# ELU's middle operation, one bit step of 16 weight pieces and a small copy moved to POOL in an attention and feed-forward kernel

## The chip, the cores and the metric

One NeuronCore of a Trainium2 chip. The time is that of one execution in device microseconds, from the first to the last instruction with what lies around it; the span in the profile is the part that the hardware profiler saw. Engines: PE multiplies matrices, DVE (VectorE), ACT (ScalarE) and POOL (GpSimd) work element by element, SP only issues transfers. Each engine takes its instructions strictly in the order in which they stand in its queue.

## The reference: windowed attention with sinks, then an ELU feed-forward layer

```python
# q, k, v: (4, 8, 768, 64); n_sink = 4, window = 128
keep = is_sink | ((rel >= 0) & (rel < window))
scores = where(keep, q @ k.T / sqrt(D), -1e9)
a = softmax(scores)            # per query row
x = (a @ v) as (3072, 512)     # 4 x 768 tokens, 8 heads x 64
h = x @ w_in                   # (3072, 2048)
g = where(h > 0, h, exp(min(h, 0)) - 1)
out = g @ w_out                # (3072, 512)
```

The weights w_in and w_out arrive as 64-bit floats.

## The kernel before: a planner writes the order of every engine

The 3072 tokens are 24 tiles of 128, in nine chunks (`SIZES`: three chunks of 2 tiles, then six of 3). Matrix products run in 16-bit floats with a high and a low part of each operand, so that one product becomes three.

**Attention** of a chunk goes head pair by head pair. PE makes the scores (L540, L541; L547 in chunks 0 and 1), DVE adds the mask and takes the row minimum (L566), ACT the exponential (L568), ACT and DVE the high and low part of the probabilities (L580, L581), POOL the four sink columns (L587 to L591), SP a transposing transfer (L599), and PE the product with v (L610, L615), from which ACT and DVE make the high and low part of x (L623, L624). v itself is split by ACT (L510) and DVE (L511); in chunks 1 to 8 ACT then copies eight rows of the low part to the place of the sinks' low part (L516).

**Weights** come in 32 pieces of 128x512; piece 2f is a column block f of w_in, piece 2f+1 the rows of w_out that belong to it. SP loads a piece as 64-bit words (L395). `weight_f32` makes 32-bit floats in four steps: ACT scales the high word (L267), DVE takes three low bits (L268), DVE the sign (L269), DVE puts all together (L270). ACT then makes the high part (L416) and POOL the low part (L417). A piece's load may be issued once the high part of the piece five before it is made (`AHEAD`).

**Feed-forward**: for each f PE makes h from x in 12 matmuls (L651, `stage1`). ACT takes exp (L659), DVE does `(e - 1) * G` (L661, ELU's middle operation), DVE takes min with 0 and max with h, which frees the bank of h (L662), ACT makes the high part of g (L664), POOL the low part (L665), and PE multiplies by w_out (L672, `stage2`), two values of f later (`LAG`). There are two banks of h. Chunks 0 and 1 run the first eight f, then both the second eight (`PARTS`), so that pieces 0 to 15 are needed first, pieces 16 to 31 only when the second halves begin. There are 9 x 16 = 144 values of f in all.

At the end, DVE checks the range of all numbers (`in_range`), PE sums the verdict over partitions (L741), DVE decides (`decide`), and all engines read the flag (L968) and branch past a general path.

**Order**: every step is a task with an engine, a planned duration and its predecessors. PE's order is fixed by positions (`pos`); from it each other task gets a due time, and a list scheduler (`Plan.forward`) puts on each engine whichever ready task is due first. `keep_order` then pins that order. So a changed duration or engine changes the order of all engines except PE. The planner models no interference between engines.

Of the kernel before, what the change touches and what calls it, by code (L numbers as in the profile page):

```python
# [15 lines left out]
AF = mybir.ActivationFunctionType  # L16
ALU = mybir.AluOpType
# [3 lines left out]
P = 128  # L21
# [71 lines left out]
class Plan:  # L93
# [162 lines left out]

def weight_f32(nc, v, d, u, raw):

    ui = u.bitcast(U16).rearrange("p (f t) -> p f t", t=2)
    words = raw.rearrange("p (f t) -> p f t", t=2)
    halves = raw.bitcast(U16).rearrange("p (f t) -> p f t", t=4)
    return (
        lambda: nc.scalar.activation(d, words[:, :, 1].bitcast(F32), AF.Copy, scale=2.0**-111),  # L267
        lambda: nc.vector.tensor_scalar(ui[:, :, 0], halves[:, :, 1], 13, None, ALU.logical_shift_right),  # L268
        lambda: nc.vector.tensor_scalar(ui[:, :, 1], halves[:, :, 3], 0x8000, None, ALU.bitwise_and),  # L269
        lambda: nc.vector.scalar_tensor_tensor(v.bitcast(I32), d.bitcast(I32), 3, u, ALU.logical_shift_left, ALU.bitwise_or),  # L270
    )
# [52 lines left out]
def fast_path(tc, ctx, first, kq, vx, wt, out, nw, flag):  # L324
# [65 lines left out]
    def weights(k):  # L390
        raw, v = raws[slot("raw")], wv[slot("wv")]

        def load():
            if wide:
                nc.sync.dma_start(raw, wt[k].bitcast(I32))  # L395
            else:
                nc.sync.dma_start(raw[:, :512].bitcast(F32), wt[k])

        def step(i):
            return lambda: weight_f32(nc, v, acc[2], wu[k % RINGS["wu"]], raw)[i]()  # L400

        ld = add("SP", 0.4, load, deps=[w_done.get(k - AHEAD, [None])[0]], lat=dma_us(P * 512 * 8))
        if wide:
            a = add("ACT", act_us(512), step(0), deps=[ld])
            u1 = add("DVE", 0.65, step(1), deps=[ld])
            u2 = add("DVE", 0.7, step(2), deps=[ld])
            b = add("DVE", 0.7, step(3), deps=[a, u1, u2])
            ring("wu", [u1, u2], [b])
            ring("wps", [a], [b])
            ring("raw", [ld], [a, u1, u2])  # L410
            first_acc2.append(b)
        else:
            a = b = add("ACT", act_us(512), lambda: nc.scalar.activation(v, raw[:, :512].bitcast(F32), AF.Copy, scale=W_SCALE), deps=[ld])
            ring("raw", [ld], [a])

        th = add("ACT", act_us(512), lambda: nc.scalar.activation(w[k][:, 0, :], v, AF.Copy), deps=[b])  # L416
        tl = add("POOL", 1.5, lambda: nc.gpsimd.tensor_tensor(w[k][:, 1, :], v, w[k][:, 0, :], ALU.subtract), deps=[th])  # L417
        ring("wv", [b], [tl])
        w_done[k] = th, tl

# [31 lines left out]
    def attention(c):  # L452
# [46 lines left out]
        for p in range(NP):  # L499
# [13 lines left out]
            ring("vs", [ld or va], [va, vb])  # L513
            if far:

                vb = add("ACT", 0.3, lambda vhi=vhi, vlo=vlo: nc.scalar.activation(vhi[64:72, nk * P :], vlo[64:72, nk * P :], AF.Copy), deps=[vb])  # L516
            ring("vhl", [va], v_users)

            po = po_ps[slot("po")]
# [114 lines left out]
    def feed_forward(c, f0, f1, start):  # L634
# [4 lines left out]
        for f in range(f0, f1):  # L639
            hp = h_ps[slot("h")]  # L640
            gf = gs[slot("g")][:, :n]
            i = slot("gh")
            gh, gl = ghs[i], gls[i]

            def stage1(hp=hp, f=f):
                win = w[2 * f].rearrange("p t (a f) -> p t a f", a=ND)
                k = 0
                for d in range(ND):
                    xh, xl = x[d][:2]
                    for part, xx in ((0, xh), (1, xh), (0, xl)):  # L650
                        nc.tensor.matmul(hp[:, :n], win[:, part, d, :], xx[:, :n], start=k == 0, stop=k == 3 * ND - 1)  # L651
# [7 lines left out]
            a = add("ACT", act_us(n) + 0.06, lambda gf=gf, hp=hp, sums=sums: nc.scalar.activation(gf, hp[:, :n], AF.Exp, scale=1.0 / G_SCALE, accum_out=sums), deps=[s1])  # L659
            exps_done.append(a)  # L660
            b = add("DVE", 0.1 + 0.0008 * n, lambda gf=gf: nc.vector.tensor_scalar(gf, gf, -1.0, G_SCALE, ALU.add, ALU.mult), deps=[a])  # L661
            b = add("DVE", dve_us(n), lambda gf=gf, hp=hp: nc.vector.scalar_tensor_tensor(gf, gf, 0.0, hp[:, :n], ALU.min, ALU.max), deps=[b])  # L662
            ring("h", [s1], [b])
            th = add("ACT", act_us(n), lambda gf=gf, gh=gh: nc.scalar.activation(gh[:, :n], gf, AF.Copy), deps=[b])  # L664
            tl = add("POOL", pool_us(n), lambda gl=gl, gf=gf, gh=gh: nc.gpsimd.tensor_tensor(gl[:, :n], gf, gh[:, :n], ALU.subtract), deps=[th])  # L665

            def stage2(order, gl=gl, gh=gh, f=f):
                def run():
                    wout = w[2 * f + 1]
                    for k, i in order:  # L670
                        gg, part = ((gh, 0), (gh, 1), (gl, 0))[k]
                        nc.tensor.matmul(acc[i], gg[:, i * P : (i + 1) * P], wout[:, part, :], start=f == f0 and k == 0, stop=f == f1 - 1 and k == 2)  # L672
# [27 lines left out]
            saved[c, i] = sto  # L700
            evacs[i] = ev

    saved, exps_done = {}, []
    start = 0
    for c, f0, f1 in PARTS:
        if f0 == 0:
# [30 lines left out]
        nc.vector.tensor_tensor(flag, flag, some[:, 0:1], ALU.mult)  # L737

    sp = s_ps[slot("s")]
    a = add("DVE", 2.0, in_range, deps=seen + exps_done)  # L740
    b = add("PE", 0.1, lambda: nc.tensor.matmul(sp[:, 0:3], ones, some16, start=True, stop=True), deps=[a], pos=start + 2 * LAG - 1.5)  # L741
    ring("s", [b], [add("DVE", 0.6, decide, deps=[b])])
    for writer, users in later:
        writer.deps.extend(users)
# [252 lines left out]
```

## Time and profile before

| | us |
|---|---|
| time, median of 3 runs (660.2 to 663.14) | 660.67 |
| the profiled execution | 662.14 |
| its span | 660.3 |
| PE busy in the span | 609.9 |
| DVE, ACT, POOL busy in the span | 458.4, 456.9, 338.2 |

PE is the busiest engine, but not evenly: in 40 slices of the span it is at 3 to 8 tenths in the first eight, at 9 in nearly all of the rest. DVE is the other way around: 9 in most of the first six slices, then 6 or 7. The profile's busy shares are averages over these two stages, so that the prediction reads windows of the span rather than the totals. In a view of groups, a row gives line, engine, operation, output<-inputs, shapes and count, then busy time in us and the mean duration of one in ns, then the engine's idle time just before them and what ended it.

### The profile page before, as it was taken

How to read it: one execution, taken by the hardware profiler on the slowest of the kernel's cores; microseconds unless marked ns; L12 is line 12 of the kernel's file. 1: busy time of each engine (PE TensorE's matmuls, PEld its weight loads, DVE VectorE, ACT ScalarE, POOL GpSimd, SP SyncE). 2: the span in 40 equal slices, each digit the busy share in tenths (PEclk: the TensorE clock that was granted, in tenths of full speed). 3: DMA queues.
4: the chain of work that ended last, by engine and by line, in shares of the span. 5: the costliest groups of instructions: out<-in, count | busy, mean ns of one | idle time of the engine just before them, and what ended most of it. 6: DMA issues, size and time to landing. Idle time of an engine off the chain costs nothing.

```text
span 660.3 us, 13443 instructions
## 1 busy us (share of the span) xinstructions
PE 609.9 (92%) x4449; PEld 370.2 (56%) x4449; DVE 458.4 (69%) x1251; ACT 456.9 (69%) x1340; POOL 338.2 (51%) x497
## 2 busy tenths in 40 slices
PE   3486799789999999999999999999999999999996
PEld 2343466456776665555555556555555565555552
DVE  6999998896677776667677776758677787524222
ACT  4999786777788887767677777766677777523221
POOL 0158866785556666544555655444446564322221
PEclk9999698899999999999999999999999999999998
DMA  7989974857654586435454566555554734211001
GB/s 264 206 282 266 276 199 144 269 142 167 145 118 128 136 184 131 116 92 171 116 152 118 133 156 167 104 111 171 112 155 128 208 84 101 49 56 49 1 0 54
DMA packets 130110, 93.41 MB, mean 141 GB/s; under 512 B 104432, under 2 KB 109552, under 8 KB 130032
## 3 DMA queue, kind: packets, MB, share of 16 engines
q1 hardware_dynamic: 130032, 92.47, 53.2%
q8 instruction: 37, 0.61, 0.4%
q14 instruction: 41, 0.34, 0.2%
HBM read 59.94 MB, written 7.34 MB: 102 GB/s over the span
## 4 chain that ended last, share of the span: by engine, by line
PE 78%; DVE 7%; ACT 5%; issue 4%; POOL 3%; DMA 3%; SPq 0%; DVEq 0%; POOLq 0%; ACTq 0%
PE h L651 33%; PE acc L672 33%; PE po L610 5%; PE s L540 3%; PE s L541 3%; DMA pt<-pq 2%; PE s L547 1%; ACT e L568 1%; DVE wu L268 1%; POOL kq L487 1%; DVE wv L270 1%; DVE wu L269 1%; DVE pq L581 1%; DVE g L661 1%; POOL kq L489 1%
## 5 line engine op out<-in xcount | busy, mean ns | idle before, releaser
L651 PE MATMUL h<-x,w 128*128 128x384 f16 (+1 forms) x1728 | 276.6, 310 | 5.6 <-DVE g L662 5.6
L665 POOL TENSOR_TENSOR gl<-g,gh 128x384 f16<-128x384 f32 (+1 forms) x144 | 126.9, 882 | 215.2 <-ACT gh L664 184.4
L651 PEld LDWEIGHTS <-w 128*128 128x128 f16 x1728 | 165.6, 99 | 98.7 <-issue 5.9
L672 PE MATMUL acc<-w,gh 128*128 128x512 f16 x768 | 195.3, 384 | 0.8 <-DVE wv L693 0.8
L661 DVE TENSOR_SCALAR g<-g 128x384 f32<-128x384 f32 (+1 forms) x144 | 65.3, 454 | 115.8 <-ACT g L659 115.3
L659 ACT ACTIVATE g<-h 128x384 f32<-128x384 f32 (+1 forms) x144 | 64.9, 451 | 88.3 <-PE h L651 83.1
L581 DVE SCALAR_TENSOR_TENSOR pq<-e,st,pq 128x256 f16<-128x256 f32 (+1 forms) x192 | 107.2, 587 | 19.7 <-ACT pq L580 19.1
L672 PE MATMUL acc<-w,gl 128*128 128x512 f16 x384 | 110.6, 383 | 0.6 <-POOL gl L665 0.4
L672 PEld LDWEIGHTS <-gh 128*128 128x128 f16 x768 | 70.9, 98 | 71.5 <-issue 3.0
L568 ACT ACTIVATE e<-e,st 128x264 f32<-128x264 f32 (+1 forms) x192 | 93.4, 487 | 11.1 <-DVE st L566 9.7
L664 ACT ACTIVATE gh<-g 128x384 f16<-128x384 f32 (+1 forms) x144 | 69.3, 481 | 44.6 <-DVE g L662 44.2
L566 DVE CUSTOM_DVE_ANT_0 e<-s,m 128x264 f32<-128x264 f32 (+1 forms) x192 | 73.0, 404 | 32.1 <-PE s L541 26.8
L580 ACT ACTIVATE pq<-e,st 128x256 f16<-128x256 f32 (+1 forms) x192 | 85.1, 480 | 10.5 <-DVE st L573 10.1
L487 POOL TENSOR_TENSOR kq<-kqs,kq 128x396 fp32r<-128x396 f32 (+1 forms) x56 | 67.2, 1199 | 23.9 <-ACT kq L483 23.0
L662 DVE SCALAR_TENSOR_TENSOR g<-g,h 128x384 f32<-128x384 f32 (+1 forms) x144 | 72.6, 504 | 1.6
L672 PEld LDWEIGHTS <-gl 128*128 128x128 f16 x384 | 37.6, 99 | 47.9 <-POOL gl L665 2.5
L483 ACT ACTIVATE kq<-kqs 128x780 fp32r<-128x780 f32 (+2 forms) x56 | 48.4, 879 | 17.1 <-PE s L541 14.3
L417 POOL TENSOR_TENSOR w<-wv,w 128x512 f16<-128x512 f32 x32 | 39.5, 1236 | 38.8 <-ACT w L416 18.9
L489 POOL TENSOR_TENSOR kq<-kqs,kq 64x384 fp32r<-64x384 f32 (+1 forms) x56 | 56.7, 1013 | 4.4
L610 PE MATMUL po<-pt,vh 128*64 128x128 f16 x704 | 41.7, 230 | 17.8 <-DMA pt<-pq 7.8
L540 PE MATMUL s<-kq 128*128 128x264 f32 x160 | 56.2, 370 | 1.7 <-POOL kq L489 1.6
L610 PEld LDWEIGHTS <-vh 128*64 128x64 f16 x704 | 31.1, 115 | 29.6 <-issue 21.7
(78 smaller groups left out, 629.2 us busy)
## 6 DMA issues: line engine op xcount, KB each, us to landing
raw<-in_wt_dram SPq DMA_DIRECT2D x32, 512.0 KB, 5.6
kqs<-in_kq_dram SPq DMA_DIRECT2D x24, 456.0 KB, 3.4
kqs<-in_kq_dram SPq DMA_DIRECT2D x24, 390.0 KB, 3.3
out_dram<-wv SPq DMA_DIRECT2D x24, 256.0 KB, 2.5
vs<-in_vx_dram SPq DMA_DIRECT2D x20, 256.0 KB, 3.1
vm<-in_vx_dram SPq DMA_DIRECT2D x6, 768.0 KB, 4.6
kqs<-in_kq_dram SPq DMA_DIRECT2D x12, 326.0 KB, 4.1
vs<-in_vx_dram SPq DMA_DIRECT2D x12, 320.0 KB, 3.1
```

The source lines that it names most:

```text
L487: nc.gpsimd.tensor_tensor(buf[:, KQ_MAX : KQ_MAX + n] if c >= DUP else buf[:, kw : 2 * kw], raw[:, :n], hi[:, :n].bitcast(F32), ALU.subtract)
L540: nc.tensor.matmul(sp[:, :wd], q, hi[:, c0 : c0 + wd], start=True, stop=False)
L566: red = add("DVE", 0.13 + 0.00145 * wd, lambda ee=ee, me=me, sp=sps[e], m=m, wd=wd: nc.vector.tensor_tensor_reduce(ee, sp[:, :wd], m[:, :w ...
L568: ex = add("ACT", 0.48 + 0.00085 * wd, lambda ee=ee, me=me, rs=rs[:, e : e + 1]: nc.scalar.activation(ee, ee, AF.Exp, bias=me, scale=-1.0, ...
L580: a = add("ACT", act_us(nb * P, True), lambda src=src, hi=hi, re=re: nc.scalar.activation(hi, src, AF.Copy, scale=re), deps=[rr])
L581: b = add("DVE", dve_us(nb * P) + 0.1, lambda src=src, hi=hi, lo=lo, re=re: nc.vector.scalar_tensor_tensor(lo, src, re, hi, ALU.mult, ALU. ...
L610: nc.tensor.matmul(po[e * D : (e + 1) * D, oc], vv[:, vo : vo + D], pt[:, (2 * e + part) * nb + i, :], start=new, stop=last)
L651: nc.tensor.matmul(hp[:, :n], win[:, part, d, :], xx[:, :n], start=k == 0, stop=k == 3 * ND - 1)
L661: b = add("DVE", 0.1 + 0.0008 * n, lambda gf=gf: nc.vector.tensor_scalar(gf, gf, -1.0, G_SCALE, ALU.add, ALU.mult), deps=[a])
L662: b = add("DVE", dve_us(n), lambda gf=gf, hp=hp: nc.vector.scalar_tensor_tensor(gf, gf, 0.0, hp[:, :n], ALU.min, ALU.max), deps=[b])
L665: tl = add("POOL", pool_us(n), lambda gl=gl, gf=gf, gh=gh: nc.gpsimd.tensor_tensor(gl[:, :n], gf, gh[:, :n], ALU.subtract), deps=[th])
L672: nc.tensor.matmul(acc[i], gg[:, i * P : (i + 1) * P], wout[:, part, :], start=f == f0 and k == 0, stop=f == f1 - 1 and k == 2)
```

## The change: three kinds of operation leave DVE and ACT for POOL

```diff
+ON_POOL = 16
...
+    if on_pool:
+        steps[1] = lambda: nc.gpsimd.tensor_scalar(ui[:, :, 0], halves[:, :, 1], 2.0**-13, -4095.5 / 8192, ALU.mult, ALU.add)
+    return steps
...
-            u1 = add("DVE", 0.65, step(1), deps=[ld])
+            u1 = add("POOL", 0.8, step(1), deps=[ld]) if k < ON_POOL else add("DVE", 0.65, step(1), deps=[ld])
...
-        tl = add("POOL", 1.5, ...L417...)
+        tl = add("POOL", 1.22, ...)
...
-                vb = add("ACT", 0.3, ...L516, nc.scalar.activation(..., AF.Copy)...)
+                vb = add("POOL", 0.32, ...nc.gpsimd.tensor_copy(...)...)
...
-            b = add("DVE", 0.1 + 0.0008 * n, ...L661, nc.vector.tensor_scalar...)
+            b = add("POOL", 0.15 + 0.00125 * n, ...nc.gpsimd.tensor_scalar...)
             b = add("DVE", ...L662...)
+            g_done.append(b)
...
-    a = add("DVE", 2.0, in_range, deps=seen + exps_done)
-    b = add("PE", 0.1, ...L741..., pos=start + 2 * LAG - 1.5)
+    a = add("DVE", 2.0, in_range, deps=seen + exps_done + g_done[-1:])
+    b = add("PE", 0.1, ..., pos=start + 2 * LAG)
```

The three low bits of pieces 0 to 15 (L268) are made by POOL, where a multiplication by 2^-13 and an addition stand for the shift; ELU's middle operation (L661) is on POOL for all 144 values of f; so is the copy of the sinks' low part (L516, 32 times). The planned duration of L417 falls from 1.5 to 1.22. The check of ranges waits for the last L662, and its matmul (L741) moves behind the last matmuls of stage 2. In the changed kernel the lines are six or seven further down: L268 on POOL is L276, L270 is L273, L417 is L423, L516 is L522, L661 is L667, L662 is L668, L665 is L672, L587 to L591 are L593 to L597.

PE's order is the same but for L741. The other engines' orders are new.

POOL at the start of its work, before: `w_132` is weight piece 0 and the pieces count up from there; `gl_114` is the low part of g for f = 0.

```order
L417 TENSOR_TENSOR w_132<-wv_120,w_132 128x512
L417 TENSOR_TENSOR w_133<-wv_121,w_133 128x512
L417 TENSOR_TENSOR w_134<-wv_122,w_134 128x512
L417 TENSOR_TENSOR w_135<-wv_123,w_135 128x512
L417 TENSOR_TENSOR w_136<-wv_120,w_136 128x512
L587 TENSOR_TENSOR st_96<-e_93,st_96 128x8
L590 CAST pq_102<-st_96 128x2x8
```

The same place after; `raw_126` to `raw_131` are the six buffers of loaded pieces, `wu` holds the low bits, `g_109` is f = 0.

```order
L276 TENSOR_SCALAR wu_125<-raw_131 128x512
L423 TENSOR_TENSOR w_135<-wv_123,w_135 128x512
L423 TENSOR_TENSOR w_136<-wv_120,w_136 128x512
L276 TENSOR_SCALAR wu_124<-raw_126 128x512
L276 TENSOR_SCALAR wu_125<-raw_127 128x512
L423 TENSOR_TENSOR w_137<-wv_121,w_137 128x512
L276 TENSOR_SCALAR wu_124<-raw_128 128x512
L667 TENSOR_SCALAR g_109<-g_109 128x256
L593 TENSOR_TENSOR st_96<-e_93,st_96 128x8
```

The low bits of up to nine pieces now stand ahead of the first ELU operation, and each stands between low parts (L423) in the one queue.

POOL later in the first halves, after: `w_143`, `w_145` are pieces 11 and 13, `g_110` and `g_109` are f = 5 and 6, `gl_116` is f = 5.

```order
L667 TENSOR_SCALAR g_110<-g_110 128x256
L522 COPY vh_87<-vl_89 8x128
L423 TENSOR_TENSOR w_143<-wv_123,w_143 128x512
L667 TENSOR_SCALAR g_109<-g_109 128x256
L423 TENSOR_TENSOR w_145<-wv_121,w_145 128x512
L672 TENSOR_TENSOR gl_116<-g_110,gh_113 128x256
```

Low parts of weights now queue behind an ELU operation that waits for ACT's exp of its f, which before they did not.

DVE at the end, before: `g_110` and `h_165` belong to the last f.

```order
L661 TENSOR_SCALAR g_110<-g_110 128x384
L725 TENSOR_SCALAR checks<-checks 128x144
L725 TENSOR_SCALAR checks<-checks 128x36
L727 TENSOR_REDUCE some<-checks 128x1 x2
L728 TENSOR_SCALAR checks<-checks 128x32
L729 TENSOR_REDUCE some<-checks 128x1
L730 TENSOR_SCALAR some<-some 128x2
L731 CAST some_204<-some 128x3
L662 SCALAR_TENSOR_TENSOR g_110<-g_110,h_165 128x384
```

And after:

```order
L668 SCALAR_TENSOR_TENSOR g_110<-g_110,h_165 128x384
L732 TENSOR_SCALAR checks<-checks 128x144
L732 TENSOR_SCALAR checks<-checks 128x36
L734 TENSOR_REDUCE some<-checks 128x1 x2
L735 TENSOR_SCALAR checks<-checks 128x32
L736 TENSOR_REDUCE some<-checks 128x1
L737 TENSOR_SCALAR some<-some 128x2
L738 CAST some_204<-some 128x3
L704 TENSOR_SCALAR wv_121<-acc_169 128x512
L704 TENSOR_SCALAR wv_123<-acc_171 128x512
L742 TENSOR_REDUCE some<-s_166 128x1
```

The check no longer stands between the two ELU operations of the last f, and the verdict (L742) comes behind the last two results.

More of the change, by code (lines that the diff above doesn't have):

```diff
@@ L254, in dma_us, with weight_f32 @@
     return nbytes / 330e3
-def weight_f32(nc, v, d, u, raw):
+def weight_f32(nc, v, d, u, raw, on_pool=False):
     ui = u.bitcast(U16).rearrange("p (f t) -> p f t", t=2)
@@ L265, in weight_f32 @@
     halves = raw.bitcast(U16).rearrange("p (f t) -> p f t", t=4)
-    return (
+    steps = [
         lambda: nc.scalar.activation(d, words[:, :, 1].bitcast(F32), AF.Copy, scale=2.0**-111),
@@ L270, in weight_f32 @@
         lambda: nc.vector.scalar_tensor_tensor(v.bitcast(I32), d.bitcast(I32), 3, u, ALU.logical_shift_left, ALU.bitwise_or),
-    )
+    ]
+    if on_pool:
+        steps[1] = lambda: nc.gpsimd.tensor_scalar(ui[:, :, 0], halves[:, :, 1], 2.0**-13, -4095.5 / 8192, ALU.mult, ALU.add)
+    return steps
 def elu(nc, g, h, scale):
@@ L399, in step @@
         def step(i):
-            return lambda: weight_f32(nc, v, acc[2], wu[k % RINGS["wu"]], raw)[i]()
+            return lambda: weight_f32(nc, v, acc[2], wu[k % RINGS["wu"]], raw, k < ON_POOL)[i]()
         ld = add("SP", 0.4, load, deps=[w_done.get(k - AHEAD, [None])[0]], lat=dma_us(P * 512 * 8))
@@ L416, in weights @@
         th = add("ACT", act_us(512), lambda: nc.scalar.activation(w[k][:, 0, :], v, AF.Copy), deps=[b])
-        tl = add("POOL", 1.5, lambda: nc.gpsimd.tensor_tensor(w[k][:, 1, :], v, w[k][:, 0, :], ALU.subtract), deps=[th])
+        tl = add("POOL", 1.22, lambda: nc.gpsimd.tensor_tensor(w[k][:, 1, :], v, w[k][:, 0, :], ALU.subtract), deps=[th])
         ring("wv", [b], [tl])
@@ L514, in attention @@
             if far:
-                vb = add("ACT", 0.3, lambda vhi=vhi, vlo=vlo: nc.scalar.activation(vhi[64:72, nk * P :], vlo[64:72, nk * P :], AF.Copy), deps=[vb])
+                vb = add("POOL", 0.32, lambda vhi=vhi, vlo=vlo: nc.gpsimd.tensor_copy(vhi[64:72, nk * P :], vlo[64:72, nk * P :]), deps=[vb])
             ring("vhl", [va], v_users)
@@ L660, in feed_forward @@
             exps_done.append(a)
-            b = add("DVE", 0.1 + 0.0008 * n, lambda gf=gf: nc.vector.tensor_scalar(gf, gf, -1.0, G_SCALE, ALU.add, ALU.mult), deps=[a])
+            b = add("POOL", 0.15 + 0.00125 * n, lambda gf=gf: nc.gpsimd.tensor_scalar(gf, gf, -1.0, G_SCALE, ALU.add, ALU.mult), deps=[a])
             b = add("DVE", dve_us(n), lambda gf=gf, hp=hp: nc.vector.scalar_tensor_tensor(gf, gf, 0.0, hp[:, :n], ALU.min, ALU.max), deps=[b])
             ring("h", [s1], [b])
+            g_done.append(b)
             th = add("ACT", act_us(n), lambda gf=gf, gh=gh: nc.scalar.activation(gh[:, :n], gf, AF.Copy), deps=[b])
@@ L701, in feed_forward @@
             evacs[i] = ev
-    saved, exps_done = {}, []
+    saved, exps_done, g_done = {}, [], []
     start = 0
@@ L739, in fast_path @@
     sp = s_ps[slot("s")]
-    a = add("DVE", 2.0, in_range, deps=seen + exps_done)
-    b = add("PE", 0.1, lambda: nc.tensor.matmul(sp[:, 0:3], ones, some16, start=True, stop=True), deps=[a], pos=start + 2 * LAG - 1.5)
+    a = add("DVE", 2.0, in_range, deps=seen + exps_done + g_done[-1:])
+    b = add("PE", 0.1, lambda: nc.tensor.matmul(sp[:, 0:3], ones, some16, start=True, stop=True), deps=[a], pos=start + 2 * LAG)
     ring("s", [b], [add("DVE", 0.6, decide, deps=[b])])
```

## Prediction, made before the changed kernel ran

> **What bounds the kernel now.** I read windows of the span first: busy time of each engine in five stretches (columns: window, its length, busy us and instruction count of PE, weight loads, DVE, ACT, POOL, then granted PE clock, DMA share, GB/s).
>
> ```profile
> 10.00:28.50 18.50, 10.70 (x64) 6.67 (x65) 16.59 (x69) 17.34 (x64) 1.16 (x1) 1.00 0.93 261
> 28.50:138.00 109.50, 86.36 (x667) 56.56 (x667) 101.30 (x238) 91.26 (x256) 77.11 (x102) 0.92 0.79 229
> 138.00:180.00 42.00, 38.58 (x308) 27.12 (x306) 31.39 (x88) 30.82 (x101) 27.10 (x42) 1.00 0.66 160
> 180.00:580.00 400.00, 399.06 (x2981) 240.43 (x2980) 280.62 (x773) 294.04 (x862) 215.04 (x319) 1.00 0.53 131
> 580.00:660.30 80.30, 74.23 (x431) 38.82 (x429) 23.56 (x58) 21.45 (x57) 16.41 (x18) 0.98 0.08 28
> ```
>
> From 180 to 580 PE is idle for 0.94 us of 400, and its order does not change, so nothing can be gained there. From 28.5 to 138 PE stands still for 23.1 us, DVE is busy for 101.3 of 109.5 (93%), POOL for 77.1 (70%). From 138 to 180 PE's idle time is 3.4 us. So the stretch from 28.5 to 138, where the weights are converted while chunks 0 and 1 run, decides. Who keeps PE waiting there (waited in all, times, longest):
>
> ```profile
> PE po L610 <- DMA pt<-pq: 6.3, 4, 2.5
> PE h L651 <- DVE g L662: 5.3, 4, 2.3
> PE po L610 <- DVE x L624: 5.2, 2, 4.1
> PE s L547 <- DVE st L566: 4.2, 5, 1.4
> PE po L610 <- ACT w L416: 2.3, 1, 2.3
> PE acc L672 <- POOL gl L665: 0.4, 1, 0.4
> ```
>
> DVE is the releaser for 5.3 + 5.2 + 4.2 = 14.7 us, transposing transfers for 6.3. The longest wait, 4.1 us, is at 62.6 to 66.7 us, and around it DVE's own operations are stretched. DVE and POOL there (start, duration, what):
>
> ```profile
> 66.56 1.12 DVE L661 TENSOR_SCALAR g<-g 128x256 f32<-128x256 f32 x1
> 67.60 1.40 DVE L269 TENSOR_SCALAR wu<-raw 128x512 uint16<-128x512 uint16 x1
> 68.89 1.40 DVE L268 TENSOR_SCALAR wu<-raw 128x512 uint16<-128x512 uint16 x1
> ...
> 66.37 3.61 POOL L417 TENSOR_TENSOR w<-wv,w 128x512 f16<-128x512 f32 x3
> ```
>
> Three DVE operations last as long as the three POOL operations beside them. Alone they are far shorter (min/median/max in ns):
>
> ```profile
> L661 DVE TENSOR_SCALAR g<-g x144: 267/360/1244, 38.0 to 648.9; 128x384 f32<-128x384 f32 x96, 128x256 f32<-128x256 f32 x48
> L268 DVE TENSOR_SCALAR wu<-raw x32: 431/464/1397, 13.9 to 137.6; 128x512 uint16<-128x512 uint16 x32
> ```
>
> So L661 went from 0.27 to 1.12 us and L268 from 0.43 to 1.40 while POOL read SBUF; POOL's three took 3.61 / 3 = 1.20 each. DVE yields, POOL hardly does.
>
> **What leaves DVE.** Groups from 28.5 to 138 us:
>
> ```profile
> L268 DVE TENSOR_SCALAR wu<-raw 128x512 uint16<-128x512 uint16 x28 | 19.2, 684 | 0.0
> L661 DVE TENSOR_SCALAR g<-g 128x256 f32<-128x256 f32 x22 | 11.5, 527 | 3.1 <-ACT g L659 3.0
> ```
>
> Of the 28 pieces in this window, 12 (pieces 4 to 15) go to POOL: 12 x 0.684 = 8.2 us. All 22 of L661 go: 11.5 us. DVE falls from 101.3 to 81.6 us, 75% of the stretch.
>
> **What POOL gets.** POOL has not run a one-input operation of this size, so its price is bounded by its rows in the same window and by the smallest one-input operation, a cast of 16 elements:
>
> ```profile
> L417 POOL TENSOR_TENSOR w<-wv,w 128x512 f16<-128x512 f32 x30 | 37.1, 1241 | 22.1 <-ACT w L416 18.9 <-DVE wu L268 1.6 <-DVE g L661 0.7
> L665 POOL TENSOR_TENSOR gl<-g,gh 128x256 f16<-128x256 f32 x22 | 17.0, 774 | 7.7 <-ACT gh L664 6.3 <-issue 1.2
> L590 POOL CAST pq<-st x64: 196/197/538, 38.4 to 573.1; 128x16 f16<-128x16 f32 x64
> ```
>
> An operation with one input lies between 0.20 us, POOL's fixed cost, and its two-input neighbour of the same length. I take the middle, since half of the reading goes away: L268 on 512 elements 0.20 + (1.24 - 0.20)/2 = 0.72 us, L661 on 256 elements 0.20 + (0.77 - 0.20)/2 = 0.49, the copy of eight rows 0.25. In this stretch that is 11 x 0.72 (piece 4 moves ahead of it, where POOL is idle) + 22 x 0.49 + about 6 x 0.25 = 20.2 us. POOL rises from 77.1 to 97.3 us, 89%. At the low ends (39 x 0.20 = 7.8) it would be 84.9 us, at the high ends (11 x 1.24 + 22 x 0.77 + 1.5 = 32.2) 109.3 us, the whole stretch.
>
> The Trainium skill (SBUF — State Buffer, section Who interferes with whom) says that one port pair is shared by VectorE and GpSimd, and that whoever starts first holds it for its whole instruction. The rows above agree (1.40 us in place of 0.43). By the page an operation that moves keeps holding the pair, only for longer (0.49 us on POOL for 0.27 on DVE), so that 22 such moves with 11 of the other kind would leave DVE's remaining two-input operations no better off; the sum by it would lose part of the gain and come to about 0 in this stretch.
>
> **The sum in the stretch.** The fullest engine was DVE with 101.3 us; it becomes POOL with 97.3. If the stretch follows its fullest engine, it shrinks by 109.5 x 4.0/101.3 = 4.3 us. POOL has to lose most of its idle time for that: 109.5 - 77.1 = 32.4 us, of which 12.2 may stay. And there is a new wait: L662 stands on DVE and now waits for POOL. Queued behind it on DVE are scores (L566) and low parts of the probabilities (L581), for which PE's attention waits; and behind L661 on POOL stand low parts of weight pieces (order rows of f = 5 and 6). I take 3.0 of the 4.3 us. Bounds: a gain of 14.7 us if all of PE's waits for DVE go, a loss of 5 if POOL's price is at its high end (109.3 us, and at least 5 us of idle time that dependences force).
>
> **Before it.** From 10 to 28.5 us POOL is idle (1.2 of 18.5) and takes the low bits of about five pieces; DVE saves 5 x 0.44 = 2.2 us of 16.6. But ACT is at 17.3 of 18.5 and the transfers at 0.93, so I count 0.5 us, between 0 and 2.2.
>
> **The dense part.** After 138 us the cover is slack in PE's order. A bank of h is free again when L662 is done, and needed three blocks of matmuls after its h:
>
> ```profile
> 640.42 1.94 PE acc L672 x9
> 642.36 1.95 PE h L651 x12
> ...
> L659 ACT ACTIVATE g<-h 128x384 f32<-128x384 f32 x96 | 47.0, 489 | 74.4 <-PE h L651 70.6 <-POOL gl L665 1.3 <-POOL st L587 1.1
> L662 DVE SCALAR_TENSOR_TENSOR g<-g,h 128x384 f32<-128x384 f32 x96 | 52.8, 550 | 1.1
> L665 POOL TENSOR_TENSOR gl<-g,gh 128x384 f16<-128x384 f32 x78 | 75.0, 961 | 125.1 <-ACT gh L664 105.8 <-issue 14.1 <-PE h L651 3.2
> L487 POOL TENSOR_TENSOR kq<-kqs,kq 128x528 fp32r<-128x528 f32 x24 | 32.1, 1339 | 12.0 <-ACT kq L483 11.8
> L489 POOL TENSOR_TENSOR kq<-kqs,kq 64x384 fp32r<-64x384 f32 x43 | 43.8, 1018 | 3.4
> ```
>
> Three blocks are 5.8 us. The chain is exp 0.49, L661 on POOL 0.20 + (0.96 - 0.20)/2 = 0.58, L662 0.55: 1.6 us, and 4.0 if L661 finds the longest pair of POOL operations (1.34 + 1.02) just begun. POOL's load from 180 to 580 becomes 215 + 78 x 0.58 + 24 x 0.25 = 266 of 400 us, 67%. So the cover holds; without it each missed bank would cost a fraction of a microsecond. I count a loss of 0.4 us, between 0 and 2.
>
> **The end.** The check runs between L661 and L662 of the last f:
>
> ```profile
> 648.92 0.36 DVE L661 TENSOR_SCALAR g<-g 128x384 f32<-128x384 f32 x1 [2.94 <-ACT g L659]
> ...
> 650.39 0.17 DVE L731 CAST some<-some 128x3 bf16<-128x3 f32 x1
> 650.47 0.55 DVE L662 SCALAR_TENSOR_TENSOR g<-g,h 128x384 f32<-128x384 f32 x1
> ...
> 652.67 0.10 PEld L672 LDWEIGHTS <-gl 128*128 128x128 f16 x1 [0.62 <-POOL gl L665]
> ```
>
> L662 starts 1.2 us after L661 ended; without the check in between, and with 0.2 us more for L661 on POOL, it starts about 1 us earlier, more than the 0.62 us that PE waits for gl. The gain is 0.6 us. The verdict now follows the last results; behind those stands their transfer to HBM, which hides the four small operations of the verdict (0.16 us each by the rows of such casts).
>
> **Sum**: -3.0 - 0.5 + 0.4 - 0.6 = -3.7 us. The profiled execution took 662.14 us (span 660.3 and 1.8 around it) and would take 658.4; it lies 1.5 above the median of 660.67. The forecast for the median is 657.0 us. A difference of 0.5%, 3.3 us, is about what a measurement of this kernel can tell from none.
>
> **Rivals.** *DVE's relief counts in full.* For it: DVE ends 14.7 of PE's 23.1 us of waits, and the clock granted in the stretch is 0.92, so that a stretch with fewer holes would also run faster. Against it: POOL's 89%. It decides if L661 on POOL costs less than 0.4 us. Three quarters of the 14.7 give -11, with the other terms -11.7: 649 us. Chance 0.20.
>
> *The transfers and the clock keep the time.* For it: 6.3 us of waits end with transposes, and the DMA share is 0.93 from 10 to 28.5; weights that are loaded earlier stand ahead of transposes in SP's queue. Then what DVE saves turns into longer waits for transfers, and only the end's 0.6 us is left: 660 us. Chance 0.25. The Trainium skill (Perfetto Trace Analysis, section Optimizing Scalar/DVE Operations) warns that moving work between these two engines "might not help", because they share a port; by it the time stays where it is, with the same 660. No run here shows it yet.
>
> *POOL becomes the bound.* Place: POOL's queue from 28.5 to 138 us, where L661 waits for exp, pieces' low parts wait behind it, and DVE waits at L662 for POOL. The price is that of the high end, 109.3 us of POOL work and 5 us of forced idle time in a stretch of 109.5: +5 us, with the dense part's upper end +2 and the end's -0.6, +6: 667 us. It decides when L661 costs above 0.6 us or L268 above 1.0. For it: POOL's rows are stretched too where DVE is busy (the cast 0.54 in place of 0.20 at most). Chance 0.22.
>
> The forecast itself keeps 0.33, and spans -6 to -2 us.
>
> **How the numbers follow.** Three quarters of the forecast's cases and all of the first rival are faster by over 0.5%: 0.25 + 0.20 = 0.45. The rest of the forecast, and nearly all of the second rival, are within: 0.08 + 0.22 = 0.30. The third rival and 0.03 of the second are slower: 0.25. The range reaches from the first rival and a little past it, 646, to the third, 667; what is left out are a gain above 14.7 and a loss above 6. The forecast's own range is 654.5 to 658.5.
>
> **What would show it.** Right: in the stretch that now runs from 28.5 to 138 us POOL at about 89% and DVE near 75%; L667 on 256 elements near 0.49 us, L276 near 0.72; PE's waits for L668 and L630 together below 8 us in place of 10.5; from 180 us on PE without gaps; the last L668 before the check, and no wait for the last gl. Wrong: PE waits for POOL (`g`, `w`) in the stretch, DVE idle in front of L668 by more than 10 us, L587 and L517 stretched further than before, or PE gaps after 180 us.

## The result and the profile after

The changed kernel took 672.54 us (median of 4 runs, 672.19 to 675.09): 1.0151 times the kernel before, with a 95% interval of 1.0125 to 1.0176. The prediction was 657.0 us, between 646 and 667. In what follows a difference in us is (ratio - 1) x 662 us, with the runs of the kernel before on the same chip as the base; for the change it is +10.0 us (8.3 to 11.7). The profiled execution took 672.19 us, with a span of 670.4.

Where the 10.1 us of span went is seen when both spans are cut at the same matmuls. The first stage 1 is 2.4 us later, the 24th (at 137.5 us before) 5.3, the 36th (178.8) 5.8, the 49th (223.8) 8.2, and from there to the last one nothing more is lost (8.1). So the windows after are taken with these shifts (columns as before).

```profile
10.00:30.90 20.90, 11.26 (x64) 7.17 (x64) 17.64 (x67) 18.08 (x64) 5.86 (x6) 1.00 0.90 249
30.90:143.30 112.40, 88.50 (x663) 56.94 (x663) 92.17 (x203) 88.49 (x247) 94.79 (x139) 0.89 0.77 218
143.30:185.80 42.50, 39.18 (x311) 27.51 (x311) 27.16 (x75) 30.99 (x100) 33.10 (x59) 1.00 0.63 158
185.80:232.00 46.20, 43.28 (x394) 30.79 (x391) 29.64 (x88) 37.45 (x122) 33.59 (x57) 1.00 0.57 140
232.00:588.10 356.10, 356.10 (x2589) 209.80 (x2588) 227.16 (x596) 250.72 (x720) 231.52 (x376) 1.00 0.53 130
588.10:670.40 82.30, 74.06 (x432) 39.00 (x429) 17.16 (x39) 21.56 (x57) 25.79 (x37) 0.96 0.06 23
```

The fourth and the fifth are two parts of the prediction's dense stretch. Before, they were:

```profile
180.00:223.80 43.80, 42.86 (x393) 30.59 (x391) 31.14 (x97) 35.93 (x119) 25.89 (x38) 1.00 0.54 132
223.80:580.00 356.20, 356.20 (x2590) 209.84 (x2589) 249.48 (x676) 258.11 (x744) 189.15 (x282) 1.00 0.53 131
```

So the six stretches were 18.5, 109.5, 42.0, 43.8, 356.2 and 80.3 us, and the losses are 2.4, 2.9, 0.5, 2.4, 0 and 2.0. In the second stretch DVE fell from 93% to 82% and POOL rose from 70% to 84%. Neither fills it, and it still became longer. PE's idle time there grew only from 23.1 to 23.9 us; the other 2.1 us stand in PE's busy time, 86.4 us for 667 matmuls before and 88.5 for 663 after, at a granted clock of 0.92 and then 0.89. Over all stretches about 3.4 of the 10.1 us are busy time of PE, the rest is idle time. Whom PE waits for from 28.5 to 180 us (waited in all, times, longest), first before and then after:

```profile
PE po L610 <- DMA pt<-pq: 7.8, 6, 2.5
PE h L651 <- DVE g L662: 5.6, 5, 2.3
PE po L610 <- DVE x L624: 5.2, 2, 4.1
PE s L547 <- DVE st L566: 4.2, 5, 1.4
...
PE acc L672 <- POOL gl L665: 0.4, 1, 0.4
```

```profile
PE h L657 <- DVE g L668: 7.7, 5, 3.8
PE po L616 <- DMA pt<-pq: 7.5, 6, 3.0
PE acc L679 <- POOL gl L672: 4.9, 2, 4.3
PE po L616 <- DVE x L630: 4.5, 2, 2.8
PE s L553 <- DVE st L572: 1.6, 4, 0.5
```

The scores' wait fell (4.2 to 1.6), as meant. But the wait for the bank of h grew (5.6 to 7.7), and that for low parts of g went from 0.4 to 4.9 us. POOL's new groups from 28.5 to 138 us:

```profile
L667 POOL TENSOR_SCALAR g<-g 128x256 f32<-128x256 f32 x21 | 10.9, 518 | 2.1 <-ACT g L665 1.7
L276 POOL TENSOR_SCALAR wu<-raw 128x512 uint16<-128x512 uint16 x11 | 9.3, 845 | 4.3 <-DVE st L579 3.0 <-DMA raw<-in_wt_dram 0.8
L522 POOL COPY vh<-vl 8x128 f16<-8x128 f16 x6 | 2.0, 333 | 0.4
```

Operations of 0.52 us (L667) are not long, and POOL is idle only 2.1 us in front of them: they find POOL busy, or waiting with something else. One f shows it (after; start, duration, what, and idle time before with its releaser):

```profile
56.71 0.37 ACT L665 ACTIVATE g<-h 128x256 f32<-128x256 f32 x1
...
57.92 1.34 POOL L423 TENSOR_TENSOR w<-wv,w 128x512 f16<-128x512 f32 x1
...
59.35 0.77 POOL L276 TENSOR_SCALAR wu<-raw 128x512 uint16<-128x512 uint16 x1
...
60.18 0.28 POOL L522 COPY vh<-vl 8x128 f16<-8x128 f16 x1
...
60.55 0.40 POOL L667 TENSOR_SCALAR g<-g 128x256 f32<-128x256 f32 x1
...
60.98 0.42 DVE L668 SCALAR_TENSOR_TENSOR g<-g,h 128x256 f32<-128x256 f32 x1 [1.81 <-POOL g L667]
61.44 0.42 ACT L671 ACTIVATE gh<-g 128x256 f16<-128x256 f32 x1 [0.69 <-DVE g L668]
...
62.84 0.77 POOL L276 TENSOR_SCALAR wu<-raw 128x512 uint16<-128x512 uint16 x1 [0.76 <-DMA raw<-in_wt_dram]
...
64.57 1.02 POOL L276 TENSOR_SCALAR wu<-raw 128x512 uint16<-128x512 uint16 x1 [0.96 <-DVE st L579]
...
67.55 1.19 POOL L672 TENSOR_TENSOR gl<-g,gh 128x256 f16<-128x256 f32 x1
...
68.79 1.03 PE L679 MATMUL acc<-w,gl 128*128 128x512 f16 x2 [4.35 <-POOL gl L672]
```

Exp is done at 57.1 us, but its 0.40 us on POOL begin at 60.55, behind a low part, low bits and the copy. DVE stands idle for 1.81 us at L668 meanwhile. The high part of g is done at 61.9, its low part begins at 67.55, since low bits of two pieces stand ahead of it, one waiting for a load and one for DVE, and the sinks' operations behind them. PE waits 4.35 us.

The end lost 2.0 us in these two executions. DVE there, before, and then DVE and the check's matmul (L748) after:

```profile
652.74 0.15 DVE L967 CAST words<-words 128x1 int32<-128x1 f32 x1
...
654.40 0.69 DVE L697 TENSOR_SCALAR wv<-acc 128x512 f32<-128x512 f32 x1 [0.60 <-PE acc L672]
```

```profile
661.99 0.17 PE L748 MATMUL s<-some,ones 128*128 128x3 bf16 x1
662.19 0.69 DVE L704 TENSOR_SCALAR wv<-acc 128x512 f32<-128x512 f32 x1 [0.60 <-PE s L748]
...
663.37 0.15 DVE L974 CAST words<-words 128x1 int32<-128x1 f32 x1
```

Before, the flag was there at 652.9 us, 7.4 ahead of the end of the span, and the last result at 655.1, 5.2 ahead of it. After, the flag is the later of the two: 663.5 us, 6.9 ahead of the end. All engines read it and branch only then, while the last transfer had landed at 664.9 us.

### The profile page after: what moved, and what is told of

Same layout as the page of the kernel before. It is cut to its first block, busy times and chain, and to the rows that moved or that the text cites. A ratio compares the mean times of both kernels' runs of the same rounds, so it can differ in the third digit from the quotient of the medians.

```text
span 670.4 us, 13441 instructions
## 1 busy us (share of the span) xinstructions
PE 613.2 (91%) x4449; PEld 371.7 (55%) x4449; DVE 416.1 (62%) x1091; ACT 449.1 (67%) x1308; POOL 426.9 (64%) x689
## 4 chain that ended last, share of the span: by engine, by line
PE 72%; POOL 8%; DMA 6%; DVE 5%; ACT 5%; issue 3%; SPq 0%; POOLq 0%; DVEq 0%; ACTq 0%
PE acc L679 32%; PE h L657 31%; PE po L616 4%; DMA raw<-in_wt_dram 3%; PE s L546 2%; DMA pt<-pq 2%; PE s L547 2%; POOL kq L495 2%; POOL gl L672 1%; ACT e L574 1%; POOL w L423 1%; POOL kq L493 1%; DVE wu L271 1%; ACT pq L586 1%; DVE pq L587 1%
## 5 line engine op out<-in xcount | busy, mean ns | idle before, releaser
L672 POOL TENSOR_TENSOR gl<-g,gh 128x384 f16<-128x384 f32 (+1 forms) x144 | 129.3, 899 | 97.2 <-ACT gh L671 89.7
L587 DVE SCALAR_TENSOR_TENSOR pq<-e,st,pq 128x256 f16<-128x256 f32 (+1 forms) x192 | 120.6, 663 | 29.0 <-ACT pq L586 28.5
L668 DVE SCALAR_TENSOR_TENSOR g<-g,h 128x384 f32<-128x384 f32 (+1 forms) x144 | 72.5, 505 | 95.7 <-POOL g L667 95.7
L665 ACT ACTIVATE g<-h 128x384 f32<-128x384 f32 (+1 forms) x144 | 65.2, 453 | 93.6 <-PE h L657 83.4
L667 POOL TENSOR_SCALAR g<-g 128x384 f32<-128x384 f32 (+1 forms) x144 | 72.3, 503 | 57.3 <-ACT g L665 53.0
L574 ACT ACTIVATE e<-e,st 128x264 f32<-128x264 f32 (+1 forms) x192 | 93.1, 486 | 12.0 <-DVE st L572 10.7
L493 POOL TENSOR_TENSOR kq<-kqs,kq 128x396 fp32r<-128x396 f32 (+1 forms) x56 | 65.2, 1165 | 15.7 <-ACT kq L489 11.4
L495 POOL TENSOR_TENSOR kq<-kqs,kq 64x384 fp32r<-64x384 f32 (+1 forms) x56 | 56.2, 1004 | 4.4
L423 POOL TENSOR_TENSOR w<-wv,w 128x512 f16<-128x512 f32 x32 | 38.9, 1217 | 10.9 <-ACT w L422 10.4
```

The costliest lines, as they stand in the source:

```text
L493: nc.gpsimd.tensor_tensor(buf[:, KQ_MAX : KQ_MAX + n] if c >= DUP else buf[:, kw : 2 * kw], raw[:, :n], hi[:, :n].bitcast(F32), ALU.subtract)
L495: nc.gpsimd.tensor_tensor(hi[D:, kc:], raw[D:, kc:], hi[D:, kc:].bitcast(F32), ALU.subtract)
L574: ex = add("ACT", 0.48 + 0.00085 * wd, lambda ee=ee, me=me, rs=rs[:, e : e + 1]: nc.scalar.activation(ee, ee, AF.Exp, bias=me, scale=-1.0, ...
L587: b = add("DVE", dve_us(nb * P) + 0.1, lambda src=src, hi=hi, lo=lo, re=re: nc.vector.scalar_tensor_tensor(lo, src, re, hi, ALU.mult, ALU. ...
L667: b = add("POOL", 0.15 + 0.00125 * n, lambda gf=gf: nc.gpsimd.tensor_scalar(gf, gf, -1.0, G_SCALE, ALU.add, ALU.mult), deps=[a])
```

## The experiments

**The check.** Two kernels: the change without its last part, and its last part alone.

```diff
-    a = add("DVE", 2.0, in_range, deps=seen + exps_done + g_done[-1:])
-    b = add("PE", 0.1, ..., pos=start + 2 * LAG)
+    a = add("DVE", 2.0, in_range, deps=seen + exps_done)
+    b = add("PE", 0.1, ..., pos=start + 2 * LAG - 1.5)
```

> The changed kernel with the range check and its matmul where they were before. If the end costs what the traces show (from the start of the last stage 1 to the end of the span 14.2 us before and 16.2 after, because the flag is read at 663.6 us, after the last results, and every engine's branch follows it), this run is about 2.0 us below the changed kernel, near 670.5 us. Rival, as the prediction had it: the transfer of the results hides the verdict; then it is within 0.5 us of the changed kernel or 0.6 us above it.

Measured: 1.0161 (1.0142 to 1.018), +10.7 us, no less than the change as a whole. The end is shorter, 15.1 us from the last stage 1 to the end in place of 16.2, but the last stage 1 came 1.3 us later in that execution. In the total it can't be seen.

> The kernel before with the range check and its matmul moved, nothing else. The flag theory: about 2.0 us above the kernel before, with the weight stretch unchanged. The prediction's step: 0.6 us below it.

Measured: 1.0025 (1.0003 to 1.0046), +1.7 us. From the last stage 1 to the end it is 15.5 us in place of 14.2, so that the moved check costs 1.4 us in the trace. But 14.2 us is the shortest of its kind: in the 17 profiled kernels whose check was not moved this part takes 14.2 to 15.4 us, 15.1 in the median, and in the three with it moved 15.4 to 16.2. The flag theory holds in sign, and the prediction's -0.6 falls. The size is less sure: 0.4 us by the medians of these traces, 1.1 by the two traces of the changed kernel, 1.7 (0.2 to 3.0) by the times, rather than 2.0.

**The large parts alone.** ELU's operation with everything else as before, and the low bits with everything else as before (the diffs are those of the change).

> The kernel before with only ELU's middle operation on POOL. Queue theory (POOL works strictly in order, so that ELU operations and low parts of g wait behind low parts of weights and of keys, and DVE waits for POOL): most of the 8.1 us by which the last stage 1 is later come from this part, +4 to +7 us. Rival: the low bits carry the loss, and this part alone lies between -2 and +1 us. The prediction's sum for this part alone would be about -2 us.

Measured: 1.0106 (1.0081 to 1.0131), +7.0 us.

> The kernel before with only the low bits of pieces 0 to 15 on POOL. Queue theory with ELU as the main part: +1 to +3 us, from the start (the first stage 1 at 37 in place of 34.6 us), where the DVE step on the same piece is stretched from 0.44 to 1.2 us beside it. Rival: this part carries the loss, +6 us or more. The prediction's sum for this part alone would be about -2 us.

Measured: 1.0015 (1.0 to 1.003), +1.0 us. So ELU's operation seemed to carry the loss. The next four asked where and how.

**Only the late chunks.**

```diff
-            b = add("POOL", 0.15 + 0.00125 * n, ...)
+            if nt == 3:
+                b = add("POOL", 0.15 + 0.00125 * n, ...)
+            else:
+                b = add("DVE", 0.1 + 0.0008 * n, ...)
```

> The kernel before with ELU's middle operation on POOL only in the six chunks of three tiles (96 of 144, from about 224 us on); in the 48 operations on two tiles it stays on DVE. Place theory (the loss comes from the stretch where weights and both first chunks are worked on; behind it the order of PE covers the longer chain): within 1 us of the kernel before. Rival (each of the 144 costs a little): two thirds of the 6 to 7 us that all 144 cost, so about +4 us.

Measured: 0.9995 (0.9972 to 1.0018), -0.3 us. 96 of the 144 operations cost nothing: from chunk 3 on the order of PE covers the longer chain.

**Order and engine apart.** A task's engine in the plan decides the order of all engines; the engine in its function decides who does the work. So one kernel keeps the orders of ELU on POOL but works on DVE, and one keeps the orders before but works on POOL.

```diff
-            b = add("POOL", 0.15 + 0.00125 * n, lambda gf=gf: nc.gpsimd.tensor_scalar(...), deps=[a])
+            b = add("POOL", 0.15 + 0.00125 * n, lambda: None, deps=[a])
...
             def middle_and_last(gf=gf, hp=hp):
+                nc.vector.tensor_scalar(gf, gf, -1.0, G_SCALE, ALU.add, ALU.mult)
                 nc.vector.scalar_tensor_tensor(...)
```

> The orders of the kernel with ELU's middle operation alone on POOL (+7 us), but the operation itself issued on DVE, straight before L668. Queue theory (the loss comes from the operation waiting in POOL's queue): most of the 7 us is gone, -1 to +2 us against the kernel before. Rival, order theory (the new plan's order on DVE, ACT, POOL and SP is worse in itself): still +5 us or more.

Measured: 1.0143 (1.0089 to 1.0198), +9.5 us. My queue theory falls as it was put: with the operation off POOL again, the orders of that plan are still 9.5 us slower. (DVE does here an operation for which that plan booked no time on DVE, so that the run does not price those orders by themselves.)

```diff
-            b = add("DVE", 0.1 + 0.0008 * n, lambda gf=gf: nc.vector.tensor_scalar(...), deps=[a])
+            b = add("DVE", 0.1 + 0.0008 * n, lambda gf=gf: nc.gpsimd.tensor_scalar(...), deps=[a])
```

> The other way about: the orders of the kernel before on all engines, but ELU's middle operation issued to POOL, at the place in POOL's queue that the plan's time gives it. Queue theory: +4 to +8 us. Order theory: within 2 us of the kernel before.

Measured: 1.006 (1.0033 to 1.0086), +4.0 us. With the orders held, the engine alone costs 4 us. So both theories have a part, and the order's is new to the account.

**What the engine's 4 us are made of.** All three kernels keep the orders before, and each leaves out part of the computation: the operation left out; work of its size on POOL, on a tile of its own; the operation on one column. The three lines with a + stand for one kernel each, in this order.

```diff
-            b = add("DVE", ..., lambda gf=gf: nc.vector.tensor_scalar(gf, gf, ...), deps=[a])
+            b = add("DVE", ..., lambda gf=gf: None, deps=[a])
+            b = add("DVE", ..., lambda: nc.gpsimd.tensor_scalar(idle[:, :n], idle[:, :n], ...), deps=[a])
+            b = add("DVE", ..., lambda gf=gf: nc.gpsimd.tensor_scalar(gf[:, :1], gf[:, :1], ...), deps=[a])
```

> The kernel before, its orders held, with ELU's middle operation left out on every engine (g becomes max(min(e, 0), h), so that part of the computation is missing). It shows what DVE's relief is worth when POOL pays nothing: 144 operations, 11.5 us of DVE's 101.3 in the weight stretch. If DVE's load sets the stretch, as the prediction had it: -4 to -11 us. If the stretch goes by chains of waits through the queues, little: 0 to -3 us.

Measured: 0.9929 (0.9893 to 0.9966), -4.7 us. That lies in the range for DVE's load (-4 to -11), but its interval, -7.1 to -2.3 us, reaches into that for the chains (0 to -3).

> Orders of the kernel before. ELU's middle operation is left out (so that part of the computation is missing); in its places in POOL's queue stands an operation of the same size on a tile of its own, for which nobody waits. The kernel without the middle operation was 5.3 us under the kernel before, with the operation on POOL it was 4.4 us above: carrying it on POOL cost 9.7. Load theory (POOL's time and the shared port cost it): this run stays near the latter, +2 to +4 us. Wait theory (DVE and then PE wait for a link of ELU's chain that stands in POOL's queue): near the former, -5 to -3 us.

Measured: 0.9987 (0.9967 to 1.0008), -0.9 us.

> Orders of the kernel before. The middle operation is on POOL but only on the first of the 256 or 384 columns (the rest of that step is missing): POOL's time goes to the fixed cost, the waits for exp and for POOL stay. Wait theory: +2 to +4 us. Load theory: -5 to -2 us.

Measured: 1.0002 (0.9984 to 1.0019), +0.1 us. (The 5.3, 4.4 and 9.7 of these expectations are differences of medians; by ratios they are 4.7, 4.0 and 8.7.) DVE's relief is worth 4.7 us when POOL pays nothing. The same work on POOL takes 3.8 of them back, the link alone 4.8, and both together, which is the operation on POOL, 8.7. Neither of the two theories of the expectations fits alone. The shares are rough: each of these differences is known to about 3 us either way, and the link on one column still takes 0.27 us of POOL's time where the whole operation took 0.48. The windows from 28.5 to 138 us, of the kernel with the operation left out, of that with work on POOL for which nobody waits, and of that with the operation on POOL:

```profile
28.50:138.00 109.50, 89.94 (x693) 58.83 (x693) 97.01 (x222) 93.56 (x263) 80.19 (x106) 0.94 0.82 234
```

```profile
28.50:138.00 109.50, 87.10 (x669) 56.12 (x669) 94.52 (x216) 91.52 (x259) 87.64 (x125) 0.92 0.79 229
```

```profile
28.50:138.00 109.50, 85.77 (x664) 57.12 (x664) 92.63 (x216) 91.84 (x256) 84.74 (x124) 0.94 0.80 229
```

PE does 693, 669 and 664 matmuls in the same 109.5 us. POOL is at 73%, 80% and 77%, far from full in each. What is lost is lost in waits. For whom PE waits from 28.5 to 180 us, in the first and the third of them:

```profile
PE po L616 <- DMA pt<-pq: 8.0, 7, 2.9
PE po L616 <- DVE x L630: 4.0, 2, 3.0
...
PE h L657 <- DVE g L668: 2.1, 2, 1.1
```

```profile
PE po L616 <- DMA pt<-pq: 9.3, 4, 3.9
PE po L616 <- DVE x L630: 7.0, 2, 5.7
PE h L657 <- DVE g L668: 4.0, 5, 1.3
```

The wait for h's bank doubles (2.1 to 4.0 us), and so nearly does that for x, which DVE makes behind the L668 that wait for POOL. The kernel with the link on one column shows the same two waits (3.7 and 7.1 us). The one with work for which nobody waits does not (1.7 and 3.9); there the transposes' wait grew instead, from 8.0 to 10.2.

**The small parts and the order.** The copy on POOL together with the planned 1.22 us for L423:

> The kernel before with the small copy on POOL and the planned 1.22 us for L423, without the three other parts. Either it is a re-deal of the orders that alone is worth some us (1 to 4 us either way), or the two small parts cost nothing (within 1 us of the kernel before), and what the three others cost adds up to the whole: 7 + 1 + 1.7 of 10.

Measured: 1.0071 (1.0046 to 1.0096), +4.7 us: two thirds of ELU's loss, from parts that I had priced at 1.5 us of POOL's time and at nothing. And all three kinds of operation on POOL with the orders of the kernel before:

> All three kinds of operation are issued on POOL, as in the changed kernel, but every order is that of the kernel before (the check isn't moved). If the plan for the new engines is worse in itself (2.6 us with the ELU operation alone), this run is 1 to 4 us below the changed kernel with its check not moved (+10.5), so near +5 to +8 us. Rival: an order that knows nothing of the new load is worse: +12 us or more.

Measured: 1.0167 (1.0134 to 1.0201), +11.1 us. With the check not moved, new orders and old ones cost the same (10.7 and 11.1); the re-plan of the whole is neither better nor worse than the old order.

Then each small part alone:

```diff
-        tl = add("POOL", 1.5, ...)
+        tl = add("POOL", 1.22, ...)
```

> The kernel before with the planned 1.22 us for L423 and nothing else: every engine does the same work, only orders differ. Order theory: all of the 4.7 us of the copy and the planned time together, since in that run PE waited 6.8 us for low parts of weights (none before), which the shorter booking lets start later. Rival: the copy on POOL costs it, and this run is within 1 us of the kernel before.

Measured: 1.0121 (1.0077 to 1.0165), +8.0 us. Every engine does the same operations as before; a number in the plan is all that differs. What PE waits for from 28.5 to 180 us, in that kernel:

```profile
PE po L616 <- DMA pt<-pq: 12.7, 8, 3.7
PE h L657 <- POOL w L423: 7.1, 5, 2.7
PE h L657 <- ACT w L422: 4.0, 3, 2.1
```

The view of the kernel before has no row of an h that waits for a weight piece; here they come to 11.1 us, and the transposes' wait grows from 7.8 to 12.7. The planner takes the booked duration off the due time, so a low part that is booked shorter is due later, and other work can come ahead of it. That these waits come about in this way is likely, but no run isolates it.

> The kernel before with the copy of the sinks' low part on POOL, booked at 0.32 us, and nothing else. Order theory: within 1 us of the kernel before (32 operations of 0.28 us). Rival: +4 us or more.

Measured: 1.0077 (1.0056 to 1.0098), +5.1 us, and not within 1 us as the order theory had it. The 32 copies have new orders behind them too, so that this run does not tell the copy from its order.

> The changed kernel with L423 booked at 1.5 us again. If the shorter booking is what it loses by: 4 us below the changed kernel, about +6. If ELU's operation carries the loss, and the booking only re-deals: within 2 us of the changed kernel, +8 to +12.

Measured: 1.014 (1.009 to 1.019), +9.3 us, the same as the change within its interval: the changed kernel does not lose by the shorter booking as such.

```diff
-            u1 = add("POOL", 0.8, ...)
+            u1 = add("POOL", 1.2, ...)
-        tl = add("POOL", 1.22, ...)
+        tl = add("POOL", 1.5, ...)
-                vb = add("POOL", 0.32, ...)
+                vb = add("POOL", 0.6, ...)
-            b = add("POOL", 0.15 + 0.00125 * n, ...)
+            b = add("POOL", 0.2 + 0.0023 * n, ...)
```

> The changed kernel, its check not moved, with POOL's operations booked long: L423 at 1.5, ELU's operation at 0.2 + 0.0023 n as its low part, the bits at 1.2, the copy at 0.6. If the loss lies in optimistic bookings: +4 us or less against the kernel before. If it lies in POOL having to carry the operations at all: +6 to +11.

Measured: 1.0303 (1.0251 to 1.0355), +20.1 us, the slowest of all. Longer bookings were no remedy; PE's waits for transposes rose to 23.1 us from 28 to 240 us (7.8 before).

**Direction or any re-deal.** L423 booked at 1.4 and at 1.6 us, with the same work.

> The kernel before with L423 booked at 1.4 us. Direction theory: +2 to +4 us, between 1.5 (0) and 1.22 (+8). Re-deal theory: anything from 0 to +8 us, and waits of PE for other things than low parts of weights.

Measured: 1.0054 (1.0035 to 1.0073), +3.6 us.

> The kernel before with L423 booked at 1.6 us, which changes the orders in only a few places. Direction theory: the kernel before or a little faster, -2 to +0.5 us. Re-deal theory: 0 to +5 us.

Measured: 1.0031 (1.0014 to 1.0048), +2.1 us. The waits of PE at 1.4, from 28.5 to 180 us, and then at 1.6:

```profile
PE po L616 <- DMA pt<-pq: 8.4, 6, 5.3
PE po L616 <- DVE x L630: 5.2, 2, 3.5
```

```profile
PE po L616 <- DVE wu L271: 5.2, 1, 5.2
PE po L616 <- DMA pt<-pq: 4.5, 2, 4.0
```

Low parts of weights are not what PE waits for most in either, and the longer booking loses too. The direction theory falls, the re-deal theory stands: three other bookings of one operation, three slower kernels (+2.1, +3.6, +8.0 us). Whether 1.5 us had been picked as the best of many bookings is not on record.

**Where each part loses.** The table gives, for the profiled execution of each kernel, how many us later than before a stage 1 begins (before: at what time), and the time from the last one to the end of the span. Each row is one execution, and those of the kernel before differ by up to 6 us from one another, so that differences of 1 or 2 us mean little.

| kernel | 1st | 24th | 49th | last | to the end |
|---|---|---|---|---|---|
| before (times) | 34.6 | 137.5 | 223.8 | 646.1 | 14.2 |
| the change | 2.4 | 5.3 | 8.2 | 8.1 | 16.2 |
| ELU's operation on POOL | -0.2 | -0.3 | 6.0 | 5.9 | 15.1 |
| the same, orders held | -0.3 | 0.0 | 2.6 | 3.0 | 15.4 |
| ELU's operation left out, orders held | -0.6 | -4.0 | -5.3 | -5.4 | 14.9 |
| low bits on POOL | 2.3 | 1.9 | 1.1 | 1.1 | 15.4 |
| copy on POOL | 1.6 | 4.7 | 5.8 | 5.8 | 15.2 |
| L423 booked at 1.22 us | 1.5 | 9.8 | 10.9 | 10.9 | 15.4 |

Up to the 24th stage 1, while the weights are converted, ELU's operation alone costs nothing in either order: the 4.0 us that DVE's relief is worth there are taken back on POOL, and no more. Its loss comes between the 24th and the 49th, where the chunks still have two tiles. PE waits there, from 137 to 230 us, 3.4 us for low parts of keys, which POOL makes (L495), and 2.6 for the bank of h; before it was 1.6 and 0.3. The copy and the booking lose nearly all of theirs up to the 24th, where they change little or no work.

## Why the prediction was wrong, point by point

**The stretch follows its fullest engine: wrong, and the step that failed.** The prediction shrank the stretch with the fullest engine (101.3 to 97.3 us), took 3.0 of 4.3 us, and forecast DVE near 75% and POOL about 89%. They came to 82% and 84%, and the stretch grew by 2.9 us. By that step POOL's new work costs nothing as long as POOL stays below what DVE had. With the orders held, ELU's operation on POOL cost 8.7 us with POOL busy at 77%, and DVE's relief was worth only 4.7. About 4.8 of the 8.7 come with the link through POOL's queue, which makes h's bank and x late, and 3.8 with POOL's time beside the others, each to about 3 us. The place was wrong too: in the profiled executions, what ELU's operation loses on balance lies behind the stretch, and losses before and in it appear with the low bits, the copy and the booking.

**The re-planned order had no price in the sum.** The prediction named the new orders, and priced only durations and one new wait. Orders alone, at the same work, cost 2.1, 3.6 and 8.0 us; the copy with its order 5.1; ELU's operation costs 7.0 with new orders and 4.0 with old ones, though these two intervals overlap a little. Nearly all of the re-dealt orders lost; why the order before is the better one is not shown. The parts alone (7.0, 1.0, 4.7 and 1.7) come to 14.4 us, more than the 10.0 of the whole: re-deals do not add up. How the 10 us of the change divide between order and engines stays open. With the old orders, the engines alone cost 11.1, and ELU's operation by itself 4.0; the low bits and the copy were not tried apart with old orders.

**The prices: nearly right.** L667 was forecast at 0.49 us and took 0.52; L276 at 0.72 and took 0.85; the copy at 0.25 and took 0.33. The rival "POOL becomes the bound" gave 667 us and came nearest, and what it said of the queue is seen in the trace of the change (L667 behind other work, DVE waiting at L668). Its price was not: it needed L667 above 0.6 us or L276 above 1.0 and POOL full, and POOL is at 84%.

**The port.** By the rule of the Trainium skill (SBUF — State Buffer, section Who interferes with whom), that whoever starts first holds the shared port pair for its whole instruction, the prediction estimated about 0 in this stretch. DVE's busy time there fell by 9.1 us, not by the 19.7 of the sum. A part of that is a misreading: DVE's records overlap a little, so that the rows of its groups before come to 118 us where its busy time is 101.3, and a row cannot be taken off whole. Most of the rest is that what stayed is stretched, as the low bits that DVE keeps (L271), from 28.5 to 138 us:

```profile
L271 DVE TENSOR_SCALAR wu<-raw 128x512 uint16<-128x512 uint16 x14 | 12.4, 885 | 0.0
```

They took 0.885 us where low bits took 0.684 before. The estimate by the rule was nearer than my sum, and still on the optimistic side.

**Before the stretch: wrong.** Forecast -0.5 us, measured +2.4. POOL was idle there as said, but the low bits alone already bring the first stage 1 to 36.9 us (34.6 before), and a re-deal without any new work to 36.1. Such a delay is partly made up later: of the 2.3 us of the low bits 1.1 are left at the 49th stage 1.

**The dense part: right from 224 us on, wrong before.** Forecast +0.4 us, at most 2, from 180 us on. Measured +2.4, all of it before 224 us, where chunk 2 still has two tiles; 0 from there on, and -0.3 us with only the late chunks moved. The prediction worked out the cover from rows with three tiles (384 columns), and for the bank of h alone. From 186 to 232 us PE waited for other things: 1.5 us for transposes and 1.4 for low parts of keys (L495), where before it waited 0.8 us, for the keys. Between 138 and 180 us 0.5 us were lost.

**The end: wrong in sign.** Forecast -0.6 us, measured +2.0 in the two traces, of which about 1 us is that the one execution before was short there, and +1.7 (0.2 to 3.0) in the times of the check moved alone. The wait for the last gl did go. But the prediction had the verdict hidden by the last transfer, and did not look at what reads it: the flag is now later than the last result, and the span ends 6.9 us behind the flag.

**The signs that it named.** PE's waits for L668 and L630 came to 12.2 us, not below 8; PE waited 4.9 us for low parts of g from POOL; L517 was stretched from 0.99 to 1.33 us. DVE's idle time in front of L668, 6.9 us, stayed under the 10 that were to show an error.

**Work moved between these two engines.** The Trainium skill (Perfetto Trace Analysis, section Optimizing Scalar/DVE Operations) says that such a move "might not help", because the two share a port. It did not help, and here it cost 1.5%; the port cannot be all of it, since orders alone cost 2 to 8 us.

No run with the whole computation was faster than the kernel before by more than its interval; the 4.7 us (2.3 to 7.1) are what could be had if the middle operation could be saved without a place on another engine.

## What to carry to other kernels

Where strict queues hand work to each other, busy shares of 90% do not say what an engine's relief is worth, nor that a less busy engine takes work for nothing: leave the operation out with all orders held, and see what its time is worth before looking for a place for it. When a planner sets the orders, hold the orders and change the engine, then change only a booked time and keep the work; the scatter of the second (here 2 to 8 us) is the error bar on a sum of durations for such a kernel. An operation with a link on each side can cost a wait in the new queue as well as its time, here roughly as much again. And cut both traces at the same matmuls, part by part, before blaming a stretch.

## What the runs showed of the hardware

POOL's operations with one input, in the changed kernel (min/median/max in ns), and ELU's on a single column, from 28.5 to 138 us:

```profile
L667 POOL TENSOR_SCALAR g<-g x144: 396/510/842, 42.6 to 657.1; 128x384 f32<-128x384 f32 x96, 128x256 f32<-128x256 f32 x48
...
L276 POOL TENSOR_SCALAR wu<-raw x16: 767/798/1060, 9.2 to 73.0; 128x512 uint16<-128x512 uint16 x16
```

```profile
L667 POOL TENSOR_SCALAR g<-g 128x1 f32<-128x1 f32 x23 | 6.0, 265 | 4.4 <-ACT g L665 1.6 <-ACT st L578 1.3 <-DVE wu L271 1.1
```

256 elements take 0.40 us at best where DVE took 0.27, 512 low bits 0.77 where DVE took 0.43, and a single column still 0.27 in the mean. At the end, the span ended 5.2 us (before) and 6.1 us (the change with its check not moved) after the last result where that came last, and 6.3 us (check moved alone) and 6.9 us (the change) after the flag where the flag came last. So the flag costs more than a result, but by how much four single executions do not tell.
